# Reordering the attention steps ahead of a mixture-of-experts chain, on one Trainium2 core

## The chip, the cores and the metric

The kernel runs on one core of a Trainium2 chip. The metric is the device time of one execution in microseconds. The kernel before took 670.33 us (median of 3 runs, 669.29 to 670.39). All inputs lie in the chip's memory, and the output goes back there.

## The reference

```python
def _attn_ref(q, k, v):                       # (2, 8, 576, 64) each
    scores = q @ k.T / sqrt(64)               # per batch and head
    mask_local = (rel >= 0) & (rel < 32)      # heads 0 to 3; rel = row - column
    mask_strided = (rel >= 0) & (column % 32 == row % 32)   # heads 4 to 7
    return softmax(where(mask, scores, -1e9)) @ v
def reference(...):
    x = attn_out as (1152 tokens, 512)
    x = sum over 4 experts of p[:, e] * (relu(x @ w1[e]) @ w2[e])     # w1 (512, 1024)
    return (sigmoid(x @ w_gate) * (x @ w_val)) @ w_out                # 1536 wide
```

Matrix products are done with operands split into a high and a low part (three products for one), in fp32r for the first expert and in fp16 after it.

## The kernel before, in words

Tokens lie in three tiles T of 384; a batch has 576 tokens, so batch 0 fills T = 0 and half of T = 1. The first expert's work is cut in "early" units: `early_up(s, T)` and `early_down(s, T)`, each four groups of 12 matmuls (`split_products`, L919). The first four units, all on T = 0, need only batch 0 of the attention. The remaining units follow, with nothing of the attention in them.

Each engine executes its instructions in the order in which the program issues them. The attention is a generator, `attention()` (L867): each `next` issues one numbered step. Steps 0 to 13 (`FIRST_GROUPS` = 14) are issued one after the other; the rest are issued inside the first four early units, 0.3 steps (`ATT_RATE`) after each triple of matmuls. `early_step` issues one step of weight preparation: a cast on ScalarE (ACT, `wh`) or a subtraction on GpSimd (POOL, `wl`).

A batch has ten attention pieces. Eight are local (here l0 to l7: 288 queries of one head each). Two are strided tiles (here s0 and s1: two heads each). Each goes through the same stages: scores on TensorE (PE), maximum on VectorE (DVE), exponent on ACT, sum and reciprocal on DVE, scaling on POOL (L103 is the line of all these, because a helper issues them), transposes on PE (L748, L823), copy out of PSUM, product with the values on PE (L762 strided, L842 local), split of the result into `xh` and `xl`. Two local pieces share one value product; l2, l3, l6, l7 issue it for themselves and their partners.

The order before comes from tables: `SEQUENCE` puts s0 at step 0, l0 to l7 at steps 1 to 8, s1 at step 9; `LOCAL` and `STRIDED` say how many steps behind the scores each stage is issued. Batch 1 has s0 at 15, s1 at 17 and l0 to l7 at 18 to 25. `EMPTY` adds matmuls on zeros (`keep_warm`, L270) to the steps. `head_start` issues the half of an early group that needs only the strided channels.

Small matmuls: a strided score tile is 128 records of 64x18 (L723), a strided value tile 128 of 18x18 (L762). PSUM tiles of the pool `gp` have four slots, shared by transposes, query and key transposes (`qkps`), zeros, strided value tiles and early groups; `op_` has one slot and `sp_` three for scores. Loads are issued by SyncE (SP) in program order, and an issue whose buffer is not free holds up the ones behind it.

Of the kernel before, what the change touches and what calls it, by code (L numbers as in the profile page):

```python
# [9 lines left out]
F32 = mybir.dt.float32  # L10
# [22 lines left out]
PSUM_BUFS = 4  # L33
PB_BUFS = 5
WARM = 11
EMPTY = {0: 4, 1: 4, 2: 4, 3: 3, **{i: 2 for i in range(4, 10)}, 10: 1, 11: 1, 12: 1, 13: 1}
T_BUFS = 4
STEP_US = dict(early_up=0.53, early_down=0.53, expert_up=0.49, expert_down=0.49, gated_up=0.25, gated_down=0.65)
MARGIN = 5.5
# [3 lines left out]
SOON = 0.9  # L43
PARK_BUFS = 4

LOCAL = (("values", 5), ("transpose", 3), ("norm", 1), ("scores", 0), ("max", 0), ("exp", 0), ("split", 5))
STRIDED = (("values", 3), ("transpose", 2), ("scores", 0), ("norm", 1), ("exp", 0), ("split", 3))
SEQUENCE = (("s", 0, 0),) + tuple(("l", 0, x) for x in range(8)) + (("s", 0, 1),)
SECOND = ((15, ("s", 1, 0)), (17, ("s", 1, 1))) + tuple((18 + x, ("l", 1, x)) for x in range(8))
FIRST_GROUPS = 14  # L50
PT_BUFS = 5
VS_BUFS = 1
WEIGHTS_FROM = 5
HEAD_START = (12, 13)
ATT_RATE = 0.3


class Ledger:
# [50 lines left out]
def attn_moe_glu_kernel(ctx, tc, q, k, v, dp, w1, w2, wg, wv, wo, out):  # L109
# [35 lines left out]

    def load_strided_qk(b, c):
        h0 = 4 + 2 * c
        both = accp.tile([NU, 2, 2, 8 * D], F32, tag="acc", name="qk01") if (b, c) == (0, 1) else None
        for x, nm in enumerate(("qs", "ks")):
            if (b, c) == (0, 1):  # L150
                qkv[nm, b, c] = both[:, x]
# [12 lines left out]
    def load_strided_v(b, c):  # L164

        h0 = 4 + 2 * c
        t = atp.tile([128, 16 * D], F32, tag="vs", name="vs", bufs=VS_BUFS)
# [13 lines left out]
    def load_vl(b, half):  # L181
        if ("vl", b) not in qkv:
            qkv["vl", b] = atp.tile([128, 4, 6, D], F32, tag="vl", name="vl")
        t = qkv["vl", b]
        i0, i1 = (1, 3) if half == 0 else (3, 6)
        if half == 0:
            nc.sync.dma_start(t[:, :, 0, :], v[b, 0:4, 0:128, :].rearrange("h p d -> p h d"))
        for h in range(4):
            src = v[b, h, 96 * i0 - 32:, :]
            win = bass.AP(src.tensor, src.offset, [[D, 128], [96 * D, i1 - i0], [1, D]])  # L190
            nc.sync.dma_start(t[:, h, i0:i1, :], win)

    raw, lands = {}, {}
    NJ = F2 // 512
# [478 lines left out]
    def qk_strided(b, c, hh):  # L673

        for nm, dst in (("qs", QT), ("ks", KT)):
# [13 lines left out]
        if (b, c, hh) == (0, 1, 1):  # L689
            acc["x2"] = accp.tile([128, KC, NTOK], F32, tag="acc", name="x2acc")  # L690
        if (b, c, hh) == (1, 1, 1):
            alloc_x(NT - 1)

# [56 lines left out]
        act.copy(t, ps)  # L750
        pt_tiles[g] = t

    def strided_values(g):
        _, b, c = g
        t, vs = pt_tiles.pop(g), qkv["vs", b, c]
        os = [(op_ if b and not j else gp).tile([128, 512], F32, tag="o" if b and not j else "g", name="o")
              for j in range(2)]
        for y in range(16):
# [6 lines left out]
        of_tiles[g] = os  # L765

    def strided_split(g):
        _, b, c = g
        for j, o in enumerate(of_tiles.pop(g)):
            ov = o[:, :16 * NA].rearrange("p (y a) -> p y a", a=NA)  # L770
            for T, off, s0, n in x_parts(b, 0, S):
                a0, a1 = s0 // 32, (s0 + n) // 32
                sel = lambda t: t[T][:, 2 + c, off:off + n].rearrange("p (a j y) -> p j y a", j=2, y=16)[:, j]
                dve.tensor_copy(sel(xh), ov[:, :, a0:a1])
                dve.tensor_tensor(sel(xl), ov[:, :, a0:a1], sel(xh).bitcast(F32), ALU.subtract)

    def local_scores(pair):

# [88 lines left out]
    def attention():  # L867
# [6 lines left out]
        locals_ = [("l", b, c, half, hh) for b in range(B) for half in range(2) for hh in range(2) for c in range(2)]  # L874
        for step, (kind, b, x) in (*enumerate(SEQUENCE), *SECOND):
            for order, (name, behind) in enumerate(STRIDED if kind == "s" else LOCAL):
                if kind == "s":
                    f = dict(values=strided_values, transpose=strided_transpose, scores=strided_scores,
                             norm=strided_norm, exp=strided_exp, split=strided_split)[name]
                    add(step + behind, order, f, (kind, b, x))  # L880
                    continue
                g = locals_[8 * b + x]
                if name in ("scores", "max"):
                    if x % 2 == 0:
                        f = local_scores if name == "scores" else local_max
                        add(step, order, f, locals_[8 * b + x:8 * b + x + 2])
                    continue
                f = dict(values=local_values, transpose=local_transpose, norm=local_norm, exp=local_exp,
                         split=local_split)[name]
                add(step + behind, order, f, g)  # L890
        for step, f, *a in ((0, qk_local, 0, 0), (1, qk_local, 0, 1), (2, qk_local, 0, 2), (7, qk_strided, 0, 1, 0),
                            (8, qk_strided, 0, 1, 1), (14, qk_strided, 1, 0, 0), (14, qk_strided, 1, 0, 1),
                            (15, qk_strided, 1, 1, 0), (16, qk_strided, 1, 1, 1), (17, qk_local, 1, 0),
                            (18, qk_local, 1, 1), (19, qk_local, 1, 2)):
            add(step, 20, f, *a)
        for x, step in enumerate(HEAD_START):
            add(step, 30, head_start, x)
        for step, n in EMPTY.items():
            add(step, 10, keep_warm, n)
        qk_strided(0, 0, 0)  # L900
        keep_warm(2)
        qk_strided(0, 0, 1)
# [389 lines left out]
    with tc.manual_schedule():  # L1292
# [2 lines left out]
        make_constants()  # L1295
        for part in range(3):
            load_local(0, part)
        load_raw_to(1)
        nc.sync.dma_start(ptok, dp.rearrange("(t p) e -> p t e", p=128))
        load_strided_v(0, 0)  # L1300
        load_vl(0, 0)
        load_strided_qk(0, 1)
        load_raw_to(2)
        load_vl(0, 1)
        for T in range(NT - 1):
            alloc_x(T)

        def attend():

            i = next(att, None)  # L1310
            if i == 4:
                load_strided_v(0, 1)
            if i == 6:
                load_raw_to(3)
            if i == 6:
                token_weights()
            if i == 7:
                spread_token_weights()
            if i == 9:
                load_p(0, 0, p00)  # L1320
            if i == 10:
                load_strided_qk(1, 0)
                load_strided_qk(1, 1)
            if i == 12:
                load_strided_v(1, 0)
                load_local(1, 0)
            if i == 13:
                load_local(1, 1)
                load_local(1, 2)
            if i == 14:  # L1330
# [12 lines left out]
        halves = job(x_half())  # L1343
# [21 lines left out]
        for n, u in enumerate(units):  # L1365
# [25 lines left out]
            if n >= N_EARLY:  # L1391
                load_p_some(n)
                load_p_some(n)
                load_some(n)
            ahead[0] = AHEAD["expert" if gated else u[0].split("_")[0]]
            if n >= N_EARLY:
                background(n)
# [47 lines left out]
```

## Time and profile before

| | |
|---|---|
| profiled execution | 669.88 us |
| its span, first to last instruction | 668.1 us |
| mean granted TensorE clock | 0.977 |
| PE busy | 650.3 us (97%) |
| DVE busy | 434.6 us (65%) |
| ACT busy | 323.0 us (48%) |
| POOL busy | 251.0 us (38%) |

Durations are of this one execution. [...] "issue" in the chain of waits is time in which an engine waited for nothing that the profile shows. Times of the trace count from the span's start.

### The profile page before, as it was taken

The numbers are of one execution on the slowest core, as the hardware profiler recorded it, in microseconds if no ns is written. First come the engines' busy times: TensorE is split into PE (matmuls) and PEld (weight loads), VectorE is DVE, ScalarE is ACT, GpSimd is POOL, SyncE is SP. The second block draws the span as 40 slices with busy tenths as digits, with TensorE's granted clock in tenths as the row PEclk, the third lists the DMA queues.
The fourth block names the chain that finished last, engine by engine and source line by source line (L and its number), as shares of the span: only waits on it lengthen the run. The fifth ranks groups of instructions, "written<-read, shape, count | busy, mean of one in ns | idle before, by whom it ended". The sixth has DMA issues, their size and how long they took to land.

```text
span 668.1 us, 13953 instructions
## 1 busy us (share of the span) xinstructions
PE 650.3 (97%) x5615; PEld 480.1 (72%) x5620; DVE 434.6 (65%) x857; ACT 323.0 (48%) x680; POOL 251.0 (38%) x282
## 2 busy tenths in 40 slices
PE   9869899999999999999999999999999999999998
PEld 5558788999876666666666666666988778977794
DVE  4735465678745288666687788898894568733432
ACT  3332324355576464678445636462557455443230
POOL 3361423000043142645044536360265566454541
PEclk9877889999999999999999999999999999999999
DMA  7558330004044064425274464434201842240002
GB/s 169 153 149 195 121 92 1 31 1 127 6 133 134 5 195 144 139 99 186 75 268 159 131 246 149 139 110 156 80 19 63 296 157 85 85 169 1 22 27 95
DMA packets 49080, 77.09 MB, mean 115 GB/s; under 512 B 20020, under 2 KB 24920, under 8 KB 47864
## 3 DMA queue, kind: packets, MB, share of 16 engines
q1 hardware_dynamic: 49016, 76.20, 36.1%
q8 instruction: 44, 0.72, 0.4%
q14 instruction: 20, 0.16, 0.1%
HBM read 59.66 MB, written 16.53 MB: 114 GB/s over the span
## 4 chain that ended last, share of the span: by engine, by line
PE 94%; DVE 3%; issue 1%; ACT 1%; POOL 0%; POOLq 0%; DVEq 0%; ACTq 0%
PE gps L923 23%; PE gps L924 22%; PE gps L925 22%; PE gps L1025 19%; PE o L762 1%; PE warm L270 1%; PE sps L792 1%; PE o L842 1%; PE qkps L702 1%; PE sps L723 1%; DVE xl L103 1%; DVE xh L103 1%; DVE nm L103 1%; PE tps L748 0%; PE tps L823 0%
## 5 line engine op out<-in xcount | busy, mean ns | idle before, releaser
L103 POOL TENSOR_TENSOR hl<-t,hh 128x384 f16<-128x384 f32 x72 | 76.6, 1067 | 180.1 <-ACT t L103 176.3
L1025 PEld LDWEIGHTS <-w 128*128 128x128 f16 x1512 | 125.0, 98 | 1.8
L1025 PE MATMUL gps<-x,w 128*128 128x192 f16 x1512 | 126.2, 246 | 0.0
L923 PE MATMUL gps<-x,w 128*128 128x384 f16 x288 | 93.9, 326 | 0.0
L924 PE MATMUL gps<-x,w 128*128 128x384 f16 x288 | 93.9, 326 | 0.0
L925 PE MATMUL gps<-x,w 128*128 128x384 f16 x288 | 93.9, 326 | 0.0
L923 PE MATMUL gps<-hh,w 128*128 128x384 f16 x288 | 93.9, 326 | 0.0
L924 PE MATMUL gps<-hl,w 128*128 128x384 f16 x288 | 93.9, 326 | 0.0
L925 PE MATMUL gps<-hh,w 128*128 128x384 f16 x288 | 93.9, 326 | 0.0
L923 PEld LDWEIGHTS <-w 128*128 128x128 f16 x576 | 56.4, 98 | 37.3 <-issue 0.2
L925 PEld LDWEIGHTS <-w 128*128 128x128 f16 x576 | 56.4, 98 | 37.2
L924 PEld LDWEIGHTS <-w 128*128 128x128 f16 x576 | 56.4, 98 | 36.4
L103 ACT ACTIVATE hh<-gps 128x384 f16<-128x384 f32 (+1 forms) x96 | 46.8, 487 | 61.4 <-PE gps L925 61.0
L103 POOL TENSOR_TENSOR stage<-magn,stage 128x512 f16<-128x512 f32 x36 | 45.5, 1273 | 45.1 <-ACT magn L103 38.9
L103 ACT ACTIVATE w<-raw,up 128x512 f16<-128x512 f32 x48 | 32.0, 715 | 34.8 <-DVE up L103 34.7
L103 DVE SCALAR_TENSOR_TENSOR w<-raw,up,w 128x512 f16<-128x512 f32 x48 | 40.1, 870 | 5.1 <-ACT w L103 4.9
L103 ACT ACTIVATE bits<-raw 128x512 f32<-128x512 f32 x36 | 24.3, 674 | 38.3 <-DVE magn L103 38.0
L924 PE MATMUL gps<-w,hh 128*128 128x512 f16 (+1 forms) x112 | 41.6, 371 | 0.0
L923 PE MATMUL gps<-w,hh 128*128 128x512 f16 (+1 forms) x112 | 41.6, 371 | 0.0
L925 PE MATMUL gps<-w,hl 128*128 128x512 f16 (+1 forms) x112 | 41.6, 371 | 0.0
L103 POOL TENSOR_TENSOR sg<-four,sg 128x384 f32<-128x384 f32 x9 | 9.9, 1098 | 80.5 <-DVE four L103 80.5
L103 DVE SCALAR_TENSOR_TENSOR t<-gps,comb,pb 128x384 f32<-128x384 f32 x36 | 22.0, 612 | 27.2 <-PE gps L925 26.6
(157 smaller groups left out, 1263.4 us busy)
## 6 DMA issues: line engine op xcount, KB each, us to landing
raw<-in_moe_w_dram SPq DMA_DIRECT2D x32, 512.0 KB
raw<-in_moe_w_gate_dram SPq DMA_DIRECT2D x12, 512.0 KB
raw<-in_moe_w_val_dram SPq DMA_DIRECT2D x12, 512.0 KB
raw<-in_moe_w_out_dram SPq DMA_DIRECT2D x12, 512.0 KB
wg<-stage SPq DMA_DIRECT2D x21, 256.0 KB
wv<-stage SPq DMA_DIRECT2D x21, 256.0 KB
w<-wg SPq DMA_DIRECT2D x3, 1024.0 KB
wo<-stage SPq DMA_DIRECT2D x12, 256.0 KB
```

Of the source, the lines that this page charges most:

```text
L103: return f(*a, **k)
L270: nc.tensor.matmul(ps, zero.to_broadcast([128, 128]), zero.to_broadcast([128, 512]), start=True, stop=True,)
L702: nc.tensor.transpose(ps[:, i * 128:(i + 1) * 128], src[:, 3 * part + i].rearrange("p j d -> p (j d)"), ident,)
L723: nc.tensor.matmul(pv_[32 * i:32 * i + NA, x, :], QT["s", b, c, hh][lo:lo + 64, rp, z, :], KT["s", b, c, hh][lo:lo + 64, rp, z, :], start= ...
L762: nc.tensor.matmul(os[j][hh * 64:hh * 64 + 64, y * NA:(y + 1) * NA], vs[r0:r0 + NA, y * D:(y + 1) * D], t[r0:r0 + NA, col:col + NA], start ...
L792: nc.tensor.matmul(pv_[:, j, :], qs_, ks_, start=False, stop=j == 2)
L842: nc.tensor.matmul(o[x * 64:x * 64 + 64, j * 96:(j + 1) * 96], lhsT, tts[x][:, j, :], start=True, stop=True)
L923: nc.tensor.matmul(ps, ah, bh, start=first and i == 0, stop=False)
L924: nc.tensor.matmul(ps, ah, bl, start=False, stop=False)
L925: nc.tensor.matmul(ps, al, bh, start=False, stop=last and i == n - 1)
L1025: nc.tensor.matmul(o, l_, r_, start=first and x + kk + y == 0, stop=last and x * kk * y == 2, skip_group_check=True)
```

## The change

Steps are listed one by one. In each batch s1 moves from behind the local pieces to step 5, between l3 and l4, and the last stage of batch 0 falls in step 12 (13 before). The strided value product is issued in two halves, in two successive steps; its two PSUM tiles are taken at the first half and given back after the second part of the split, two steps later. The strided split goes by token tile, and its copy into `xh` moves from DVE to ACT. s1's queries, keys and values of batch 0 get space of their own (`stead`), so that its values can be loaded without a wait for s0's; the buffer of the result `x2` is taken later. Several loads move ahead, others back. Zeros per step fall from 31 matmuls in all to 19. Weight preparation in steps 5 to 12 goes at two steps each (16 in all, as before, but evenly). `ATT_RATE` falls from 0.3 to 0.25, and batch 1 starts at step 14.

```diff
-EMPTY = {0: 4, 1: 4, 2: 4, 3: 3, **{i: 2 for i in range(4, 10)}, 10: 1, 11: 1, 12: 1, 13: 1}
+EMPTY = {0: 3, 1: 2, 2: 2, 3: 1, 4: 2, 5: 1, 6: 1, 7: 1, 8: 1, 9: 1, 10: 1, 11: 2, 12: 1}
-FIRST_GROUPS = 14
+SECOND = 14
+FIRST_GROUPS = 13
-HEAD_START = (12, 13)
-ATT_RATE = 0.3
+HEAD_START = (10, 11)
+ATT_RATE = 0.25
...
-    def strided_values(g):
+    def strided_values(g, half):
...
+        if half == 0:
+            of_tiles[g] = [
+                (op_ if b and not j else gp).tile([128, 512], F32, tag="o" if b and not j else "g", name="o")
+                for j in range(2)]
+        os = of_tiles[g]
+        for y in range(8 * half, 8 * half + 8):
...
-    def strided_split(g):
+    def strided_split(g, part):
+        T, off, s0, n = list(x_parts(b, 0, S))[part]
...
-                dve.tensor_copy(sel(xh), ov[:, :, a0:a1])
-                dve.tensor_tensor(sel(xl), ov[:, :, a0:a1], sel(xh).bitcast(F32), ALU.subtract)
+            act.copy(sel(xh), ov[:, :, a0:a1])
+            dve.tensor_tensor(sel(xl), ov[:, :, a0:a1], sel(xh).bitcast(F32), ALU.subtract)
...
+        for b in range(B):
+            z = SECOND * b
+            ls = [("l", b, c, half, hh) for half in range(2) for hh in range(2) for c in range(2)]
+            for c, at in ((0, z), (1, z + 5)):
+                g = ("s", b, c)
+                add(at, 30, strided_scores, g)
+                add(at, 50, strided_exp, g)
+                add(at + 1, 10, strided_norm, g)
+                add(at + 2, 60, strided_transpose, g)
+                add(at + 3, 60, strided_values, g, 0)
+                add(at + 4, 60, strided_values, g, 1)
+                add(at + 4, 90, strided_split, g, 0)
+                add(at + 5, 90, strided_split, g, 1)
+            exps = (1, 2, 3, 4, 6, 7, 8, 9)
+            turns = (4, 5, 6, 7, 9, 10, 10, 11)
+            for x, g in enumerate(ls):
+                if x % 2 == 0:
+                    add(z + exps[x], 30, local_scores, ls[x:x + 2])
+                    add(z + exps[x], 40, local_max, ls[x:x + 2])
+                add(z + exps[x], 50, local_exp, g)
+                add(z + exps[x] + 1, 20, local_norm, g)
+                add(z + turns[x], 10, local_transpose, g)
+            for x, at in ((2, 7), (3, 8), (6, 11), (7, 12)):
+                add(z + at, 5, local_values, ls[x])
+                add(z + at, 90, local_split, ls[x])
+            for part in range(3):
+                add(z + part, 80, qk_local, b, part)
+            for hh in range(2):
+                add(z + 3 + hh, 80, qk_strided, b, 1, hh)
+                if b:
+                    add(z - 1, 80, qk_strided, b, 0, hh)
         for x, step in enumerate(HEAD_START):
-            add(step, 30, head_start, x)
+            add(step, 95, head_start, x)
         for step, n in EMPTY.items():
-            add(step, 10, keep_warm, n)
+            add(step, 70, keep_warm, n)
...
+        load_strided_v(0, 0)
+        load_strided_qk(0, 1)
         load_raw_to(1)
+        load_vl(0, 0)
+        load_raw_to(2)
+        load_strided_v(0, 1)
+        load_vl(0, 1)
         nc.sync.dma_start(ptok, dp.rearrange("(t p) e -> p t e", p=128))
...
-            for _ in range((i >= WEIGHTS_FROM) + (i >= WEIGHTS_FROM + 4) + (i in (11, 12))):
+            for _ in range(2 * (i >= WEIGHTS_FROM)):
                 early_step(0)
```

The second argument of `add` orders the calls inside a step.

## Rows read from the trace of the kernel before

**Rows 1.** The page's 40 equal slices: granted TensorE clock in tenths.

```profile
PEclk9877889999999999999999999999999999999999
```

**Rows 2.** Busy time by stretch: PE, PEld, DVE, ACT, POOL (instructions), clock, DMA share, GB/s.

```profile
8.00:17.00 9.00, 8.53 (x231) 6.49 (x234) 4.88 (x14) 4.35 (x17) 1.50 (x2) 1.00 0.81 162
17.00:35.50 18.50, 15.12 (x199) 9.60 (x194) 13.31 (x38) 8.30 (x40) 7.30 (x8) 0.91 0.54 140
35.50:50.30 14.80, 8.91 (x282) 7.55 (x282) 4.53 (x13) 4.13 (x8) 9.04 (x9) 0.66 0.62 166
50.30:54.95 4.65, 4.25 (x22) 2.75 (x21) 3.93 (x12) 0.00 (x0) 0.00 (x0) 0.50 0.64 143
54.95:120.90 65.95, 62.33 (x888) 56.22 (x888) 35.45 (x93) 22.58 (x79) 21.16 (x24) 0.90 0.36 95
120.90:668.10 547.20, 543.91 (x3983) 393.85 (x3981) 369.91 (x682) 281.55 (x533) 208.39 (x226) 1.00 0.34 114
```

**Rows 3.** Chain that ended last, 35 to 55 us: start, duration, what.

```profile
35.60 1.21 PE sps L723 x80
...
38.84 1.26 POOL wl L103
...
43.93 3.32 PE o L762 x116
47.25 2.51 issue
```

**Rows 4.** The same chain, 16 to 22 us.

```profile
16.27 2.04 PE o L762 x122
...
19.37 0.22 issue
...
20.30 1.02 DVE nm L103 x2
...
21.73 0.02 issue
```

**Rows 5.** DVE's groups by form, 8 to 55 us: busy us, mean ns, idle before.

```profile
L103 DVE COPY PT<-tps 128x288 f32<-128x288 f32 x8 | 3.5, 439 | 0.9 <-PE tps L823 0.9
...
L103 DVE CAST xh<-o 128x192 fp32r<-128x192 f32 x5 | 2.3, 450 | 9.5 <-PE o L762 9.5
...
L103 DVE CAST xh<-o 128x96 fp32r<-128x96 f32 x5 | 1.5, 300 | 0.0
```

**Rows 6.** ACT's groups in the same stretch.

```profile
L103 ACT COPY PTs<-tps 128x512 f32<-128x512 f32 x2 | 1.2, 586 | 3.1 <-PE tps L748 3.1
...
L103 ACT ACTIVATE qsT<-qkps 128x288 f32<-128x288 f32 x2 | 0.8, 410 | 0.0
```

**Rows 7.** The tile `ss` (strided sums), 0 to 100 us: ns minimum, median, maximum.

```profile
L103 DVE TENSOR_SCALAR ss<-ss x4: 174/458/1273, 11.8 to 78.0; 128x16 f32<-128x16 f32 x4
```

**Rows 8.** Busy time around the clock's falls; columns of Rows 2.

```profile
36.90:40.30 3.40, 1.10 (x8) 0.76 (x7) 3.26 (x8) 1.47 (x3) 1.60 (x2) 1.00 0.79 220
40.30:57.30 17.00, 13.16 (x171) 10.57 (x173) 5.55 (x18) 2.66 (x5) 6.85 (x6) 0.50 0.65 168
...
74.50:77.90 3.40, 3.17 (x10) 2.74 (x9) 1.39 (x3) 0.65 (x2) 1.28 (x1) 0.50 0.18 47
77.90:81.35 3.45, 3.45 (x144) 2.97 (x144) 0.57 (x4) 0.00 (x0) 1.90 (x2) 0.99 0.38 134
81.35:84.75 3.40, 3.40 (x14) 3.40 (x14) 3.30 (x9) 2.03 (x8) 0.70 (x1) 0.50 0.22 68
...
91.20:94.60 3.40, 3.40 (x21) 3.19 (x18) 2.67 (x7) 1.15 (x6) 0.00 (x0) 0.55 0.55 98
```

**Rows 9.** PE's waits, 54.95 to 120.9 us: total us, times, longest.

```profile
PE qkps L702 <- issue: 1.9, 1, 1.9
PE tps L748 <- POOL wide L103: 1.2, 1, 1.2
```

**Rows 10.** The chain of waits again, one matmul of an early group.

```profile
57.66 0.17 PE gps L924
```

More of the change, by code (lines that the diff above doesn't have):

```diff
@@ L44 @@
 PARK_BUFS = 4
[L46 to L49, printed above, removed]
-FIRST_GROUPS = 14
+SECOND = 14
+FIRST_GROUPS = 13
 PT_BUFS = 5
-VS_BUFS = 1
 WEIGHTS_FROM = 5
-HEAD_START = (12, 13)
-ATT_RATE = 0.3
+HEAD_START = (10, 11)
+ATT_RATE = 0.25
 class Ledger:
@@ L147, in load_strided_qk @@
         h0 = 4 + 2 * c
-        both = accp.tile([NU, 2, 2, 8 * D], F32, tag="acc", name="qk01") if (b, c) == (0, 1) else None
         for x, nm in enumerate(("qs", "ks")):
             if (b, c) == (0, 1):
-                qkv[nm, b, c] = both[:, x]
+                qkv[nm, b, c] = stead[:NU, 16 * D * x:16 * D * (x + 1)].rearrange("p (h x) -> p h x", h=2)
             elif (b, c) == (1, 1):
@@ L166, in load_strided_v @@
         h0 = 4 + 2 * c
-        t = atp.tile([128, 16 * D], F32, tag="vs", name="vs", bufs=VS_BUFS)
+        if (b, c) == (0, 1):
+            t = stead[:, 32 * D:48 * D]
+        else:
+            t = atp.tile([128, 16 * D], F32, tag="vs", name="vs")
         for x in range(4):
@@ L191, in load_vl @@
             nc.sync.dma_start(t[:, h, i0:i1, :], win)
+    stead = accp.tile([128, KC * NTOK], F32, tag="acc", name="stead")
     raw, lands = {}, {}
@@ L688, in qk_strided @@
                 dve.tensor_copy(t, pv_)
-        if (b, c, hh) == (0, 1, 1):
-            acc["x2"] = accp.tile([128, KC, NTOK], F32, tag="acc", name="x2acc")
         if (b, c, hh) == (1, 1, 1):
@@ L751, in strided_transpose @@
         pt_tiles[g] = t
-    def strided_values(g):
+    def strided_values(g, half):
         _, b, c = g
[L755 to L758, printed above, removed]
+        t, vs = pt_tiles[g], qkv["vs", b, c]
+        if half == 0:
[4 more added lines that the diff above has]
+        for y in range(8 * half, 8 * half + 8):
             for j in range(2):
@@ L764, in strided_values @@
                         vs[r0:r0 + NA, y * D:(y + 1) * D], t[r0:r0 + NA, col:col + NA], start=True, stop=True)
-        of_tiles[g] = os
-    def strided_split(g):
+    def strided_split(g, part):
         _, b, c = g
-        for j, o in enumerate(of_tiles.pop(g)):
+        T, off, s0, n = list(x_parts(b, 0, S))[part]
+        for j, o in enumerate(of_tiles[g]):
             ov = o[:, :16 * NA].rearrange("p (y a) -> p y a", a=NA)
-            for T, off, s0, n in x_parts(b, 0, S):
-                a0, a1 = s0 // 32, (s0 + n) // 32
-                sel = lambda t: t[T][:, 2 + c, off:off + n].rearrange("p (a j y) -> p j y a", j=2, y=16)[:, j]
-                dve.tensor_copy(sel(xh), ov[:, :, a0:a1])
-                dve.tensor_tensor(sel(xl), ov[:, :, a0:a1], sel(xh).bitcast(F32), ALU.subtract)
+            a0, a1 = s0 // 32, (s0 + n) // 32
+            sel = lambda t: t[T][:, 2 + c, off:off + n].rearrange("p (a j y) -> p j y a", j=2, y=16)[:, j]
+            act.copy(sel(xh), ov[:, :, a0:a1])
+            dve.tensor_tensor(sel(xl), ov[:, :, a0:a1], sel(xh).bitcast(F32), ALU.subtract)
     def local_scores(pair):
@@ L872, in add @@
             work.setdefault(step, []).append((order, len(work.get(step, ())), f, a))
[L874 to L895, printed above, removed]
+        for b in range(B):
[29 more added lines that the diff above has]
+                    add(z - 1, 80, qk_strided, b, 0, hh)
@@ L1310, in attend @@
             i = next(att, None)
-            if i == 4:
-                load_strided_v(0, 1)
             if i == 6:
                 load_raw_to(3)
[L1315 to L1321, printed above, removed]
+            if i == 8:
                 load_strided_qk(1, 0)
                 load_strided_qk(1, 1)
+            if i == 9:
+                token_weights()
+                load_strided_v(1, 0)
+            if i == 10:
+                spread_token_weights()
+                load_local(1, 0)
             if i == 12:
-                load_strided_v(1, 0)
-                load_local(1, 0)
-            if i == 13:
+                load_p(0, 0, p00)
                 load_local(1, 1)
                 load_local(1, 2)
-            if i == 14:
+            if i == 13:
                 load_vl(1, 0)
@@ L1394, in attn_moe_glu_kernel @@
                 load_some(n)
+            if u == ("early_down", 0, 0):
+                acc["x2"] = accp.tile([128, KC, NTOK], F32, tag="acc", name="x2acc")
             ahead[0] = AHEAD["expert" if gated else u[0].split("_")[0]]
```

5 lines of the change are left out of this document (removed).

## Prediction

> **What bounds the kernel now.** I read the page's slices first: the granted clock stands at 9 in tenths from the seventh slice on, and the lower digits are all in the first six, some 100 of 668 us [rows 1]. Then the busy time by stretch: from 120.9 us to the end PE is busy 543.91 of 547.20 us at clock 1.00 [rows 2]. That stretch holds nothing of the attention, and its weights are prepared against its own units, so I take it as a block that starts earlier or later. All that the change can move is when the block starts. Ahead of it lie two stages. Stage A, batch 0, runs to the first full early group at 54.95 us; stage B, the four early units with batch 1 among them, takes 65.95 us.
>
> In stage A two engines take turns as the bound. From 17.0 to 35.5 us DVE is busy 13.31 of 18.50 us; from 35.5 to 50.3 only 4.53 of 14.80, and PE 8.91 [rows 2]. The chain of waits says why: s1 comes last and alone. Its scores end at 36.8, its scaling stands behind a weight subtraction on POOL (38.84 to 40.10), its transposes and values then run at clock 0.50 (116 records of the value tile in 3.32 us, against 122 in 2.04 at 16.27), and inside the values PE stands still for 2.51 us with nothing to wait for [rows 3, 4, 8]. I read that stillness as the fetch of PE's own instructions: the value tile is 128 matmuls and 128 weight loads in a row. The same happens for 1.9 us in stage B [rows 9].
>
> In stage B PE is busy 62.33 of 65.95 us, at mean clock 0.90 [rows 2]: the loss is mostly clock.
>
> **The change, stage A.** *DVE's sum.* Before, DVE did 4.88 + 13.31 + 4.53 + 3.93 = 26.65 us in 8 to 54.95 us [rows 2]. The move to ACT takes away four copies of 192 columns and four of 96 in batch 0: 4 x (0.45 + 0.30) = 3.0 us [rows 5]. l7's split, which before lay behind 54.95, belongs to the stage: two copies and two subtractions of about those sizes, 1.5 us. That leaves 25.1 us, 4.9 of it done by 17 us [rows 2]. The rest, 20.2 us in some 58 instructions with 0.03 us between neighbours (an estimate from the 0.02 between two of them in the chain [rows 4]), is 22 us of DVE without a wait.
>
> *Where DVE resumes.* Before, the maxima of l2 and l3 start at 20.30, because their scores are behind the whole value tile (2.04 us) and the wait of 0.22 [rows 4]. The value halves now stand behind the scores, so the maxima start near 20.3 - 2.3 - 0.2 = 17.8. Floor for DVE's last instruction of the stage: 39.8.
>
> *DVE's waits.* I walked the queues step by step in the new order with the durations of these rows. DVE idles for 1.2 us in step 4 (key transposes behind half a value tile and two zeros), 0.9 in step 5 (s1's exponent), 1.25 in step 8 (scores of l6, l7 behind the values of l3, which need the one slot that l2's split gives back), 1.25 in step 9 (s1's `xh` on ACT behind two exponents), 1.1 in steps 11 and 12, and 1.05 in small pieces: 6.75 in all. DVE ends at 46.6, and early_up, which needs only l7's first part, could start 1.1 earlier, at 45.5.
>
> *What the walk leaves out.* First, slots. The two value tiles are now held for two steps, so two of gp's four slots serve all transposes; head_start at step 10 then waits for s1's second split. A wait is at most one copy and one transpose, 0.44 us [rows 5] and about as much for the transposes (an estimate: three records, where three of an early group take 3 x 0.17 [rows 10]); two such waits show in the tail, 2 us; bounds 0 (all hidden) and 8 (one in each of nine steps). Second, POOL. A sum of 16 columns on DVE takes 174 ns, and 1273 at worst, when it meets a weight subtraction (1.26 us) on POOL [rows 3, 7]. Before, half of the subtractions ran while DVE was idle; now all eight run beside it, with some seven such sums. I take 0.5 us that isn't hidden, bounds 0 and 7 x 1.1. Third, instruction fetch: s1's scores (256 records in 1.2 us) follow half a value tile in step 5, with the DMA queues full (share 0.81 and 0.54 in the two stretches [rows 2]). I take 0.5, bounds 0 and 2.51 [rows 3].
>
> [...]
>
> So early_up starts at 45.5 + 2 + 0.5 + 0.5 = 48.5 instead of 54.95: **6.5 us**. Ends: 38.7 with no wait at all (16 us saved), and 45.5 + 8 + 7.7 + 2.5 = 63.7 with every bound against it at once (9 us lost).
>
> *At no cost.* ACT's eight copies per batch of 0.41 to 0.59 us each [rows 6] lie in 8.30 + 4.13 us busy of 33.3 [rows 2]; without that cover they would cost 4 us. Twelve zeros fewer give PE back time that it waits away anyhow. The loads: the initial ones all stand ahead of s1's values (about 34 us in the walk), and the DMA share of 0.54 in 17 to 35.5 [rows 2] shows room; SP then carries batch 1's queries, keys and values past the weight loads, for use from step 13 on. If a load were late, its step waits for it whole, some 3 us. `x2`'s later buffer waits only for s1's values, done ten microseconds earlier.
>
> **Stage B.** The clock is 0.50 in 74.50 to 77.90 and in 81.35 to 84.75 [rows 8], and mostly in 91.20 to 94.60; each costs half of 3.4, 1.7 us. The first follows PE's stillness. Before the second, in 77.90 to 81.35, PE was busy 3.45 of 3.45 us, but with one whole value tile and small local matmuls, no early group [rows 8]; the third is alike. With halves, four triples of an early group (12 x 0.17 = 2.1 us [rows 10]) stand between them. I count both away: 3.4 us. The stillness and its clock, 1.9 + 1.7 = 3.6, came right behind a strided score tile; where it falls depends on how the tile lies in the fetched blocks, and scores aren't cut: half of it, 1.8. The 1.2 us for s0's scaling [rows 9] shrink as steps come every four triples instead of 3.3: 0.6. Against these: in step 22 s1's first half takes the single slot of `op_` one step after l3's values took it, and PE waits until DVE has made the maxima of l6 and l7, 1.02 us [rows 4], and the copies of l3's split, 0.7 [rows 5]: 1.7 us. Sum: 3.4 + 1.8 + 0.6 - 1.7 = **4.1 us**; ends 9.4 (all clock and waits gone, the 1.2 us of half clock at 54.95 to 57.3 too) and -2.
>
> Together 10.6 us: 669.88 - 10.6 = 659.3. The profiled execution lies 0.45 under the median of the runs shown, so **659.7**; this case's own range is 653 to 663.
>
> **Rivals.** *Halves don't hold the clock.* If what counts isn't the small matmuls, the falls at 81.35 and 91.2 come back: 10.6 - 3.4 = 7.2 saved, 663.1. For it: PE at 0.50 also followed a stretch with 1.10 of 3.40 us busy [rows 8], so idle time does it too, and I can't tell the causes apart. Against it: no wait of PE in 77.9 to 81.35.
> [...]
>
> *Half clock in stage A.* PE has fewer zeros and waits of up to 3 us (in the walk, 25.9 to 28.8, for s1's chain on DVE). If the clock falls there and stays, PE's 19 us of steps 4 to 12 (my sum) take 1.7 times as long (as the value tile's records [rows 3, 4]); early_up starts near 53, and 2 + 4.1 are saved: 664.2. Against it: the mean clock was 0.91 in 17 to 35.5, where PE waited for 3.4 us in all [rows 2].
>
> *Slower: PSUM slots.* The value tiles are held through three steps, four times (steps 3 to 5, 8 to 10, 17 to 19, 22 to 24): twelve steps in which transposes, key tiles and, in stage B, early groups queue for the slots that are left. It decides from 1.05 us a step on beyond what I counted (12.6 us). At 1.2 us, a little over one copy and transpose for each, stage A loses 6 more, stage B 8: 4 slower, 673.7. Against it: in stage B only one of the two tiles lies in gp.
>
> *More.* DVE near its floor and stage B without falls: 10 + 9: 651.
>
> **How the numbers follow.** Forecast 0.48, halves 0.18, half clock 0.12, slots 0.13, more 0.09. The range 651 to 668 takes in all but the slots and half of the outer edges. A difference under 0.2% (1.3 us) can't be told from none by these runs. Faster 0.82, same 0.06 (half-clock case at its bad end, slots at its mild end), slower 0.12.
>
> **What would show it.** The first early_up matmul near 48.5 and the first unit on T = 1 (120.9 before) near 110. L762 in groups of 64, with no stillness inside; clock 1.00 behind steps 18 and 23; DVE without a gap of 9.5 us before `xh` [rows 5]; ACT issuing that copy; PE waiting some 1.7 us ahead of the seventh L762 group. It is wrong if early_up starts behind 53, if waits for copies out of PSUM head PE's list, or if the last stretch is longer than 547.2 us.

## The result, and the profile after

The changed kernel takes 663.86 us (median of 9 runs, 659.38 to 666.49), the one before 670.33 beside it (9 runs, 668.57 to 671.37): ratio 0.9907, interval 0.9879 to 0.9935. It is faster by 6.5 us. The profiled execution took 659.38, 10.5 less than before's 669.88, and it is the shortest of the nine; so its trace shows what the change can do, not what it does on the median. The median, 663.86, lies outside the 653 to 663 that the forecast gave as its own range. A second profiled execution of the same kernel (the first experiment) took 663.17, and the difference between the two is told there.

The page's slices of granted clock in the changed kernel, against [rows 1]: lower digits in slices 2, 3 and 6, where they filled slices 2 to 6.

```profile
PEclk9679989999999999999999999999999999999999
```

Busy time by stretch in the changed kernel, with the columns of [rows 2]; the cuts lie at the first matmul of `early_up` (48.14 us) and at the first unit on T = 1 (110.0).

```profile
8.00:17.00 9.00, 8.17 (x191) 6.20 (x178) 5.72 (x16) 4.42 (x18) 2.32 (x3) 1.00 0.88 213
17.00:35.50 18.50, 16.03 (x344) 11.83 (x339) 10.03 (x30) 8.55 (x35) 7.00 (x8) 0.72 0.50 124
35.50:48.10 12.60, 10.59 (x155) 7.90 (x148) 6.69 (x25) 5.89 (x21) 8.49 (x8) 0.73 0.85 211
48.10:110.00 61.90, 58.08 (x883) 52.01 (x882) 33.16 (x85) 24.73 (x87) 21.41 (x24) 0.97 0.41 107
110.00:657.30 547.30, 543.96 (x3983) 393.91 (x3981) 370.47 (x683) 281.58 (x533) 208.03 (x225) 1.00 0.34 114
```

Stage A shrank from 54.95 to 48.1 us, stage B from 65.95 to 61.9, and the last stretch stayed at 547.3 [rows 2]. In the profile of before, 2.51 of those 54.95 us were the stillness inside s1's values [rows 3]; the first profile of the changed kernel has none in stage A, so without stillness the stage went from 52.4 to 48.1. The chain of waits in stage A, where [rows 3] showed s1 alone, now runs, behind the load of s1's keys, through DVE, ACT and PE in turns:

```profile
10.59 7.74 DMA stead<-in_k_dram
18.46 0.49 PE qkps L681 x4
...
33.67 0.46 PE sps L784 x2
34.13 0.88 PE sps L792 x12
35.01 0.55 DVE nm L99
35.64 1.00 ACT P L99 x5
36.76 0.61 ACT wh L99
37.36 1.05 ACT P L99 x6
38.42 0.38 ACT xh L99
38.82 0.88 DVE xl L99 x2
```

PE's waits in stage B of the changed kernel (columns of [rows 9]) have one long entry without a releaser, and the timeline shows where it is: L763, the first half of s1's values in step 22, starts 1.58 us late, when DVE has done two maxima and two copies into `xh` (start, duration, instruction, idle time before it).

```profile
PE o L763 <- issue: 1.6, 1, 1.6
PE gps L932 <- ACT hh L99: 1.1, 1, 1.1
PE gps L932 <- ACT qsT L99: 0.7, 2, 0.5
```

```profile
89.66 0.40 ACT L99 COPY of<-o 128x288 f32<-128x288 f32 x1 [1.41 <-PE o L842]
...
90.85 1.02 DVE L99 TENSOR_REDUCE nm<-sps 96x3 f32<-96x384 f32 x2 [1.61 <-PE sps L792]
...
91.79 0.51 DVE L99 CAST xh<-o 128x192 fp32r<-128x192 f32 x2
...
92.39 1.12 PE L763 MATMUL o<-PTs,vs 18*64 18x18 f32 x64 [1.58 <-issue]
```

Behind that wait PE runs at half clock once:

```profile
93.90:97.20 3.30, 3.30 (x12) 3.20 (x12) 0.00 (x0) 0.00 (x0) 0.00 (x0) 0.50 0.07 17
```

That is one fall in stage B where [rows 8] had three after the stage's first microseconds.

### The profile page after: what moved, and what is told of

Same layout as the page of the kernel before. It is cut to its first block, busy times and chain, and to the rows that moved or that the text cites. A ratio compares the mean times of both kernels' runs of the same rounds, so it can differ in the third digit from the quotient of the medians.

```text
span 657.3 us, 13924 instructions
## 1 busy us (share of the span) xinstructions
PE 644.1 (98%) x5608; PEld 475.6 (72%) x5608; DVE 428.7 (65%) x841; ACT 327.3 (50%) x696; POOL 250.9 (38%) x282
## 4 chain that ended last, share of the span: by engine, by line
PE 92%; DVE 2%; ACT 2%; SPq 1%; DMA 1%; issue 1%; POOL 0%; ACTq 0%; POOLq 0%; DVEq 0%
PE gps L932 23%; PE gps L933 23%; PE gps L934 23%; PE gps L1034 19%; DMA stead<-in_k_dram 1%; SPq L177 1%; PE o L842 1%; PE o L763 1%; ACT P L99 1%; PE sps L792 1%; PE tps L823 0%; DVE ss L99 0%; PE qkps L681 0%; DVE xl L99 0%; PE warm L270 0%
## 5 line engine op out<-in xcount | busy, mean ns | idle before, releaser
L932 PE MATMUL gps<-x,w 128*128 128x384 f16 x288 | 93.9, 326 | 0.0
L933 PE MATMUL gps<-x,w 128*128 128x384 f16 x288 | 93.9, 326 | 0.0
L934 PE MATMUL gps<-x,w 128*128 128x384 f16 x288 | 93.9, 326 | 0.0
L932 PE MATMUL gps<-hh,w 128*128 128x384 f16 x288 | 93.9, 326 | 0.0
L933 PE MATMUL gps<-hl,w 128*128 128x384 f16 x288 | 93.9, 326 | 0.0
L934 PE MATMUL gps<-hh,w 128*128 128x384 f16 x288 | 93.9, 326 | 0.0
L99 POOL TENSOR_TENSOR stage<-magn,stage 128x512 f16<-128x512 f32 x36 | 45.5, 1273 | 45.1 <-ACT magn L99 38.9
```

Source lines behind the costliest of these rows:

```text
L99: return f(*a, **k)
L932: nc.tensor.matmul(ps, ah, bh, start=first and i == 0, stop=False)
L933: nc.tensor.matmul(ps, ah, bl, start=False, stop=False)
L934: nc.tensor.matmul(ps, al, bh, start=False, stop=last and i == n - 1)
```

## The experiments

Edits are against the changed kernel unless said otherwise. "Fetch" stands for PE standing still in a run of small matmuls, or right behind one, with nothing to wait for; that it is the fetch of instructions is a reading, taken up in the second experiment. Ratios are to the kernel before, run beside each experiment: its median was 669.15 us beside the control, the halves together, the split from the copy and the zeros, 670.87 beside the fetch, ACT's copies, s1's place and the scores in halves, and 671.33 beside the rest. A difference of two medians from different groups can be off by some 2 us for that reason.

### What differs between two executions of one kernel

The changed kernel again, with no edit; it serves as the control of the others.

> The changed kernel itself once more, as the control of this call. Its runs so far lie between 659.4 and 666.5 us, and their granted clock between 0.984 and 0.974. Theory (the spread is clock): the time without half of the time at 0.50, span x (1 - (1 - clock)), is the same within 2 us in all runs (646 to 650 us so far), and a profile of a slower run shows more stretches at 0.50 ahead of 110 us. Rival (something else varies, a load or a wait): that corrected time varies as much as the time itself.

Measured: 663.81 (661.47 to 666.13), ratio 0.9918 [0.9888, 0.9947]. Stage A took 51.98 us, 3.8 more than in the other profile; stage B 61.85. PE's timeline and the two totals by stretch (columns of [rows 2]) show the difference:

```profile
21.77 0.62 PE L763 MATMUL o<-PTs,vs 18*64 18x18 f32 x14 [1.18 <-issue]
...
29.15 0.45 PE L721 MATMUL sps<-ksT,qsT 64*18 64x18 f32 x28 [2.77 <-issue]
```

```profile
0.00:21.20 21.20, 18.56 (x342) 12.67 (x344) 9.73 (x26) 9.02 (x33) 6.81 (x19) 0.95 0.85 207
0.00:27.50 27.50, 22.82 (x469) 15.96 (x471) 11.58 (x32) 10.14 (x36) 7.63 (x20) 0.84 0.85 196
51.95:113.80 61.85, 58.02 (x883) 52.01 (x882) 32.05 (x85) 24.76 (x87) 21.44 (x24) 0.97 0.42 110
```

PE stood still for 1.18 + 2.77 = 3.95 us, once after 686 records (matmuls and weight loads) and once after 940, and not at all there in the first profile. 51.98 - 3.95 = 48.0: apart from fetch both executions have the same stage A.

Of the expectation neither side held. Span times granted clock, an estimate of the time without the half of the stretches at 0.50, lies between 646.4 and 649.9 in the nine runs and these four: a spread of 3.5 us, not within 2, where the spans spread by 7.1. But it accounts for three of the four slowest runs (666.05 to 666.13): their clock is 0.974, and 664.0 x 0.974 = 646.7 against 657.3 x 0.984 = 646.8 for the shortest. So fetch makes the difference between the two profiles, and half clock much of that between other runs; where it lies in those, no profile shows.

### Is it the fetch of instructions?

The kernel before, with three warm-up matmuls fewer and 32 of eight columns more, so that all later instructions lie 58 records further on.

```diff
-WARM = 11
+WARM = 8
...
+        tiny = gp.tile([128, 512], F32, tag="g", name="tiny")
+        for _ in range(32):
+            nc.tensor.matmul(
+                tiny[:, :8], zero.to_broadcast([128, 128]), zero.to_broadcast([128, 8]), start=True, stop=True)
```

> The kernel before with 32 matmuls of 8 columns on zeros in place of 3 of 512 in the warm-up: PE's program is 58 records longer ahead of everything, at about the same time. Theory (the stillness inside s1's values is instruction fetch, at a fixed count of PE's records): before it came behind 116 of the tile's 128 matmuls; now it comes 58 records, 29 matmuls, earlier, behind about 87, and the one behind the strided scores of stage B moves in among them. Rival (a load or a buffer ends it): it stays behind 116 matmuls. If the DMA queues happen to be free, it may be too short to be seen.

Measured: 669.99 (one run). `early_up` started at 58.02, 54.5 without the two stalls, where the kernel before has 52.4. The stillness moved, but not by 58 records: it left s1's values and stood in s0's values (L762) and s1's scores (L723). PE's timeline and the totals to those points, then the totals to the two points of the kernel before:

```profile
21.48 0.83 PE L762 MATMUL o<-PTs,vs 18*64 18x18 f32 x21 [2.23 <-issue]
...
42.28 0.27 PE L723 MATMUL sps<-ksT,qsT 64*18 64x18 f32 x12 [1.26 <-issue]
```

```profile
0.00:20.50 20.50, 16.76 (x344) 11.56 (x345) 6.56 (x20) 6.45 (x20) 6.03 (x18) 0.95 0.81 181
0.00:41.90 41.90, 33.90 (x596) 22.42 (x596) 20.56 (x61) 14.76 (x60) 13.42 (x26) 0.88 0.56 134
```

```profile
0.00:48.50 48.50, 39.24 (x717) 26.80 (x721) 25.27 (x70) 18.89 (x68) 21.49 (x33) 0.88 0.67 162
0.00:73.90 73.90, 60.41 (x1095) 45.09 (x1101) 37.83 (x101) 26.15 (x85) 28.47 (x39) 0.86 0.68 166
```

The forecast of the place failed, and what came in its stead says more. Matmuls and weight loads together, the stillness stood at 689 and 1192 here, at 1438 and 2196 before, at 686 and 940 in the control: neighbours 254, 252 and 246 apart, the last step 758, three times 253. The other profiles agree: their thirteen stalls of 0.5 us or more stand at 684 to 688, at 938 to 942 and at 1440 records. The same counts pass without a stall in other executions (in the first profile of the changed kernel and in that of the split from the copy). One packet of 0.02 MB on the queue that the profile calls "instruction" starts in the stall or within some 3 us ahead of it, in each of the five stalls of the kernel before, of the control and of the whole tile without a wait (below), as here in the DMA view of the kernel before, 47.2 to 49.8 us:

```profile
q8 instruction: 1, 0.02, 2.5%
```

Over the whole span that queue has 44 packets in the profile of before and 44 in the first one of the changed kernel, for 11235 and 11216 matmuls and weight loads: one for some 255 records, and the stalls stand on a grid of some 252. They lasted 0.5 to 5.2 us. Such packets also come where PE doesn't stall (one between 17.0 and 18.5 us of the changed kernel's first profile). So the counts and the packets speak for fetch; why it is late in one execution and not in another, no run shows.

### Do the halves hold the clock?

Both halves in one step, behind one another:

```diff
-                add(at + 4, 60, strided_values, g, 1)
+                add(at + 3, 60, strided_values, g, 1)
```

> The second half of each strided value product is issued right behind the first, in the same step; all else as in the changed kernel. Theory (halves hold the clock in stage B): falls to 0.50 follow the two value tiles of batch 1, 1.7 us each, and 3 to 4 us are lost against the control; a stillness inside a tile may add to it. Rival (halves don't hold the clock, the falls come from waits): the time of the control within 1 us, or less, since the split can start a step earlier in effect.

Measured: 666.26 (664.83 to 666.42), ratio 0.9950 [0.9934, 0.9965]: 2.4 us of the gain gone. Stage B 64.25, but the clock held at 1.00 behind s0's whole tile (74 to 81 us) and fell to 0.50 from 97.0 to 103.6, behind the 1.58 us wait and s1's whole tile:

```profile
74.00:81.00 7.00, 5.74 (x40) 5.28 (x39) 3.11 (x9) 2.24 (x10) 0.82 (x1) 1.00 0.23 76
97.00:103.60 6.60, 6.60 (x84) 6.46 (x77) 0.37 (x2) 0.31 (x2) 0.00 (x0) 0.50 0.04 10
```

So one of the two falls that the theory named came, and it lasted longer. Wait and whole tile came together there, so the same edit was made again with the wait removed (its edit is the next experiment's):

> e3 with the value tiles whole: both halves in one step, but no wait for the op_ slot. In e2 the clock fell behind s1's whole tile of batch 1, which followed a wait of 1.58 us, and not behind s0's. Theory now (the tile alone does not bring the clock down, the wait with it does): no fall in stage B, 58 to 60 us for the stage as in e3 (58.6); any loss against e3 lies in stage A. Rival (the prediction's: whole tiles bring it down): falls behind one or both, stage B 1.7 to 5 us longer.

Measured: 663.04 (661.65 to 665.81), ratio 0.9894 [0.9858, 0.9930]. Stage B 61.45 with one fall, at 0.50 from 98.5 to 101.9 us, behind s1's whole tile and with PE not idle ahead of it. In stage A one stall of 5.20 us inside the whole tile of s0 (start, duration, instruction, idle time):

```profile
23.97 0.18 PE L763 MATMUL o<-PTs,vs 18*64 18x18 f32 x1 [5.20 <-issue]
...
95.58 0.90 PE L792 MATMUL sps<-klT,qlT 64*96 64x128 f32 x12
96.41 2.06 PE L763 MATMUL o<-PTs,vs 18*64 18x18 f32 x128
98.39 0.63 PE L932 MATMUL gps<-xh,wh 128*128 128x384 f32 x1
```

```profile
53.25:114.70 61.45, 58.16 (x883) 51.77 (x882) 32.73 (x85) 24.61 (x87) 21.38 (x24) 0.97 0.39 108
```

So the halves hold the clock at s1: stage B's mean clock is 1.00 in the next experiment and 0.97 here. At s0 the clock holds with a whole tile too (1.00 from 74 to 81 us above), so there they do nothing for it. Against the next experiment they are worth 61.45 - 58.60 = 2.85 us in stage B, 1.8 of it PE's busy time and 1.0 its waits. With the slot's wait in place they are worth 64.25 - 61.90 = 2.35. These are differences between one profile each.

### What the slot of `op_` costs

In the local splits of batch 1, DVE's copy into `xh` reads ACT's copy of the result (`of`) instead of the PSUM tile, so that the slot comes free once ACT has copied. In batch 0 nothing changes, because there `of` is the PSUM tile itself.

```diff
-            dve.tensor_copy(dh, o[:, p0:p0 + n])
+            dve.tensor_copy(dh, of[:, p0:p0 + n])
```

> In the local split of batch 1, DVE's copy into xh reads the SBUF copy `of` in place of the PSUM tile, so that the tile of op_ is given back when ACT has copied it. Theory (the 1.58 us of stillness at 90.82 are the wait for that slot, not instruction fetch): it goes, because the slot is free at about 90.06, before the maxima; 1.6 us saved, and up to 1.7 more if the fall of the clock at 93.9 goes with it: 1 to 3.5 us under the control. Rival (it is a fetch): it stays at 1.6 us in the same place. DVE's copies from SBUF may meet POOL and take longer, which would cost nothing on PE.

Measured: 660.74 (656.12 to 662.25), ratio 0.9879 [0.9854, 0.9905]. Its profile has stage A 48.10 without fetch, and stage B:

```profile
48.10:106.70 58.60, 56.34 (x883) 50.38 (x881) 32.66 (x85) 24.69 (x87) 21.40 (x24) 1.00 0.42 113
```

The wait is gone, and with it the half clock: 3.3 us less than 61.90, of which 1.58 is the wait and half of 3.30, 1.65, the clock. That the wait ended with the slot is thereby shown; the profile itself had named no releaser. The other profiles agree: the wait of 1.58 us stands in all seven profiles of the changed kernel and its versions in which DVE reads the PSUM tile, and in none of the five in which it reads the copy.

### Zeros against the half clock of stage A

```diff
-EMPTY = {0: 3, 1: 2, 2: 2, 3: 1, 4: 2, 5: 1, 6: 1, 7: 1, 8: 1, 9: 1, 10: 1, 11: 2, 12: 1}
+EMPTY = {0: 4, 1: 4, 2: 4, 3: 3, **{i: 2 for i in range(4, 12)}, 12: 1}
```

> 32 matmuls on zeros in batch 0's steps in place of 19 (4, 4, 4, 3, then 2 a step), at the places of the changed kernel. Theory (stage A is bound by DVE and waits, and PE at half clock costs in its last part): clock 1.00 for more of 18 to 46 us, early_up 1 to 3 us earlier than 48.1 in a run like the one shown, the spread smaller. Rival (PE is itself near the bound in stage A, busy 12.5 of 14.5 us): early_up 1 to 3 us later, the 13 extra zeros at 0.22 to 0.43 us each standing in front of the attention's matmuls.

Measured: 662.73 (660.03 to 665.26), ratio 0.9901 [0.9869, 0.9933], not to be told from the control. Half clock in stage A fell from 17.1 to 13.6 us; stage A took 49.79, with 2.54 of fetch. So early_up would have started at 47.3 without fetch, 0.8 earlier than in the control. In stage B the clock stayed at 0.50 from 94.3 to 108.0 behind the slot's wait, where 93.9 to 97.2 was all before, and the stage took 66.15 us in place of 61.9:

```profile
94.30:108.00 13.70, 13.63 (x160) 12.84 (x155) 3.44 (x12) 3.04 (x12) 1.33 (x3) 0.50 0.08 12
```

The edit leaves batch 1 alone, so the length of this fall is a second term, of up to 4 us, that differs between executions.

### ACT's copies

```diff
-            act.copy(sel(xh), ov[:, :, a0:a1])
+            dve.tensor_copy(sel(xh), ov[:, :, a0:a1])
```

> The strided split's copy into xh goes back from ACT to DVE, all else as in the changed kernel (control 663.8 us). Theory (DVE bounds stage A): 3.0 us more work on DVE in batch 0, of which what stands in gaps is hidden; early_up 1.5 to 3 us later, 665 to 667. Rival (ACT's queue is the later one: the subtraction waited 1.31 and 0.72 us for the copy behind two exponents): the same or up to 1 us faster.

Measured: 663.90 (662.49 to 665.35), ratio 0.9904 [0.9868, 0.9940]. Stage A 51.37 with 0.68 + 2.77 of fetch, 47.9 without: the move from DVE to ACT is worth nothing that shows, as the rival had it.

### s1's place in batch 0

s1's scores in step 9, behind the local pieces; batch 1 two steps later (edit cut to its core; `head_start` and a load of batch 1 move along, and two zeros come on top).

```diff
-            for c, at in ((0, z), (1, z + 5)):
+            for c, at in ((0, z), (1, z + (5 if b else 9))):
...
-            exps = (1, 2, 3, 4, 6, 7, 8, 9)
-            turns = (4, 5, 6, 7, 9, 10, 10, 11)
+            exps = (1, 2, 3, 4, 6, 7, 8, 9) if b else (1, 2, 3, 4, 5, 6, 7, 8)
+            turns = (4, 5, 6, 7, 9, 10, 10, 11) if b else (4, 5, 6, 7, 8, 9, 9, 10)
```

> In batch 0 alone s1 goes back behind the local pieces (step 9, its split in 13 and 14), l4 to l7 a step earlier, batch 1 from step 16 on; halves, loads, ACT copies, rate and batch 1's order as in the changed kernel; the same 16 steps of weight preparation. Theory (s1's place is the largest term of stage A): its chain stands alone at the end again, early_up 4 to 7 us later than in the control, 668 to 671 us in all. Rival (halves and loads made the gain): within 1.5 us of the control's 663.8.

Measured: 672.0, 673.2, 673.6 and 662.44; with runs so far apart no ratio is given. In the profile (672.0) stage A took 56.68, with 3.3 of fetch, so 53.4 without, and stage B 66.15:

```profile
PE o L763 <- issue: 3.3, 2, 1.6
PE o L842 <- DVE xl L99: 3.0, 1, 3.0
```

```profile
56.65:122.80 66.15, 62.49 (x881) 56.14 (x881) 31.00 (x81) 24.79 (x87) 21.42 (x24) 0.89 0.28 81
```

By this one trace s1's place is worth 53.4 - 48.1 = 5.3 us of stage A, all of the 4.3 that the stage gained without fetch (52.4 to 48.1) and more. Stage B has the order of the changed kernel; its 66.15 us are the long fall once more, at 0.50 from 101.4 to 115.1. The total isn't settled: one run of four was ten microseconds shorter.

### Strided scores in halves, and what adds up

The 128 records of a strided score tile are issued by head; s1's first head goes one step earlier. With the free slot of `op_`:

```diff
+            if hh != part:
+                continue
...
-                add(at, 30, strided_scores, g)
+                add(at - c, 30, strided_scores, g, 0)
+                add(at, 30, strided_scores, g, 1)
```

> e3 (the local split reads the SBUF copy) with the strided scores cut too: s1's 64 matmuls of the first head are issued a step earlier than those of the second, in both batches. Theory (the spread of stage A is instruction fetch: 1.18 us inside the half value tile and 2.77 inside s1's scores in the control's profile): 256 records in 1.2 us become twice 128 two microseconds apart, the stillness inside the scores goes or shrinks under 1 us; median 1 to 3 us under e3's 660.7. Rival (the fetch is late because the queues are full, whatever PE issues): the stillness moves to another place and keeps its size; the time of e3 within 1 us.

Measured: 658.34 (657.1 to 663.73, 6 runs), ratio 0.9842 [0.9801, 0.9882]. Fetch 0.71 + 0.52 in stage A (50.17), stage B 58.75 at clock 1.00; both stalls are under 1 us, as the theory had it. The same edit without the free slot:

> The changed kernel with the strided scores in halves, the local split reading PSUM again. Separates the two parts of e8. If fetch and slot wait are two terms that add up: the control's 663.8 less e8's step against e3 (2.4 us), 661 to 662, with the wait of 1.6 us in front of s1's first half in batch 1. If e8's step came from something else: 663 to 664.

Measured: 661.67 (660.62 to 661.78), ratio 0.9868 [0.9843, 0.9894]; fetch 2.16, the slot's wait and the fall back, stage B 61.8. By the medians the two edits add up: about 2 us for the scores (663.81 to 661.67), about 3 for the slot. For the slot the stages B show it (58.6 to 59.1 us without the wait, 61.8 to 62.1 with it and 66.15 with the long fall behind it). For the scores the traces don't show how: the stall of 2.16 stood inside the first half of s1's scores, and fetch in stage A was 1.06 to 2.19 us in the four profiles with halved scores against 0 to 3.95 in the six with whole scores and halved value tiles.

With the scores in halves, the free slot and the zeros of the earlier experiment:

> e8 (scores in halves, split from the SBUF copy) with the 32 zeros of e4. Theory (in stage A half clock costs on the way to early_up): the stretches at 0.50 ahead of 48 us shrink from some 20 us to 13, as in e4, and early_up comes 1 to 2 us earlier than e8's 50.2; median 656 to 658. Rival (the zeros stand in front of what the path needs, and add records to the fetched blocks): e8's 658.3 or up to 2 us more.

Measured: 657.87 (655.76 to 661.2, 6 runs), ratio 0.9819 [0.9792, 0.9847]. This is the fastest version, ahead of both kernels; the interval overlaps that without the zeros, so what these add is open. In its profile, the longest of the six runs, early_up started at 53.03 with 2.19 of fetch, later and not earlier than 50.17. Last, weight preparation from step 4 instead of 5 (without the zeros):

```diff
-WEIGHTS_FROM = 5
+WEIGHTS_FROM = 4
...
-            for _ in range(2 * (i >= WEIGHTS_FROM)):
+            for _ in range(2 * (WEIGHTS_FROM <= i < 12)):
```

> e8 with the 16 steps of weight preparation in steps 4 to 11 in place of 5 to 12. Theory (the transposes of l6 wait 1.3 us for a scaling that stands behind a weight subtraction on POOL, and ACT's copies behind casts): POOL and ACT are freer at the end of stage A, early_up 0.5 to 1.5 us earlier, 657 to 658. Rival (the same queues are only blocked a step earlier, at s1's chain): the same or up to 1 us slower.

Measured: 660.70 (657.27 to 663.54), ratio 0.9857 [0.9827, 0.9887]: no gain that shows. Stage A took 53.22 with 1.06 of fetch, the clock at 0.50 from 23.5 to 50.8 us without a break.

## Why the prediction was right, and where it was not

*The number.* In the first profile stages A and B shrank by 6.8 and 4.05 us, against 6.5 and 4.1 forecast, and its time came within 0.1 us of the 659.3 forecast for a profiled execution. That is partly luck: it is the shortest of nine runs and has no fetch in stage A. The median, 4.2 us over the forecast, lies beside the 663.1 and 664.2 of the two rivals on the clock, though neither of these is what the traces show, as told below.

*The block.* Right: the last stretch is 547.20 before and 547.30 after, so all of the gain is an earlier start.

*Stage B, 4.1 us.* 65.95 - 61.90 = 4.05, and 4.10 in the control. Split into waits and clock the forecast holds too: its terms for waits come to 1.7 less half of 1.9 and less 0.6, next to nothing, and PE's waits went from 3.62 to 3.82 us while its busy time fell from 62.33 to 58.08. The single parts came less close. Clock 1.00 behind step 18; behind step 23 one fall remained, and the row of 3.30 us at 0.50 shows it. The stillness of 1.9 us and s0's wait of 1.2 [rows 9] are gone whole, more than the 1.8 + 0.6 counted. The slot wait, forecast at 1.7 in step 22, was 1.58 in that place. Not counted were waits of early groups for ACT, 1.1 + 0.7 us, and the fall behind the slot's wait. The half clock at the stage's start, 1.2 us, went too and stood only in the ends. So errors of some 1 to 2 us each cancelled. The case that halves don't hold the clock is half refuted: it is true of s0, false of s1. For the price, the two stages B without the slot's wait differ by 2.85 with one fall, against 3.4 forecast for two; and the fall behind a whole tile (0.50 from 98.5 to 101.9 us) came with no wait of PE's from 93.7 us on, as that at 81.35 came behind 3.45 us busy of 3.45 [rows 8].

*Stage A, 6.5 us.* Forecast start of `early_up` 48.5; 48.14 in the first profile, 51.98 in the control. The step that failed is the third of "what the walk leaves out": fetch "I take 0.5, bounds 0 and 2.51". What it measured:

| kernel | early_up starts | fetch | difference |
|---|---|---|---|
| changed, first profile | 48.14 | 0 | 48.1 |
| changed, control | 51.98 | 3.95 | 48.0 |
| halves together | 51.17 | 3.03 | 48.1 |
| split from the copy | 48.10 | 0 | 48.1 |
| copies on DVE | 51.37 | 3.45 | 47.9 |
| scores in halves alone | 50.47 | 2.16 | 48.3 |
| whole tile, no wait | 53.29 | 5.20 | 48.1 |
| scores in halves, free slot | 50.17 | 1.23 | 48.9 |
| more zeros | 49.79 | 2.54 | 47.3 |
| scores in halves, free slot, zeros | 53.03 | 2.19 | 50.8 |
| scores in halves, free slot, weights earlier | 53.22 | 1.06 | 52.2 |

The changed kernel, its control and the split from the copy have one and the same stage A, and give 48.0 to 48.1 without fetch, against 48.5 - 0.5 = 48.0 forecast: the walk's sum stands. The next four lie within 0.4 us of one another; the last four do not, and three of them change the zeros or the weights of the stage. The term itself is 0 to 5.2 us, one or two stalls of 0.5 to 3 each and once one of 5.2. I had bounded it by the one stall seen in the trace of before; the shifted run of that kernel had 2.23 + 1.26 in its stage A, so the bound was too low there already. With 3.95 in place of 0.5 the forecast would be 663.1, and the median is 663.86. The nine runs have no profile each, so that fetch makes their whole spread (659.4 to 666.5) isn't shown, and their clocks speak against it; the control shows it for the 3.8 us between the two profiled executions. The second term that differs between executions, the length of the fall behind the slot's wait (3.3 to 13.7 us), the prediction had put at nothing.

*Right sum, wrong split.* "DVE's sum" had DVE busy for 20.2 us from 17 us on, and its walk had it idle for 6.75. It was busy 10.03 + 6.69 = 16.72 of 31.1 us and so idle for some 14. PE was busy 26.62 of 31.1, at a mean clock of 0.72: nearer to the bound than DVE. So the rival "half clock in stage A" did occur in its clock (about 17 us at 0.50), without its price: `early_up` started at 48.1, not near 53. The run with weights earlier comes near that price: there the clock stayed at 0.50 for 27.3 us, and `early_up` started at 53.22, 52.2 without fetch. Whether the clock or the weights' place did it, that run can't tell. The copies on ACT, which I counted as 3.0 us off DVE, brought nothing when put back, as befits an engine with that much idle time. That errors in DVE's work and DVE's waits cancelled is luck of the walk, not a confirmation of DVE as the bound. By its chain the stage is bound by the alternation shown above; more zeros, or the copies put back on DVE, each move it by under what the runs can tell.

*At no cost.* Nearly: the load of s1's keys stands in the chain with 7.74 us and held PE for 0.6 us. POOL's term was small, near the 0.5 taken: `ss` took 982 ns at worst (1273 in [rows 7]), some 0.8 more than its 174, and the eight of the local pieces' sums 164 on average.

```profile
L99 DVE TENSOR_SCALAR ss<-ss x4: 174/536/982, 11.0 to 83.0; 128x16 f32<-128x16 f32 x4
```

*PSUM slots.* The slower rival did not come: of waits for the four slots of `gp` the longest in stage A is 0.6 us, zeros behind a copy of `PT`, where the forecast had taken 2. But one of the signs of error did appear: waits for a slot that DVE still reads head PE's list, 1.3 us in stage A (l3's values behind l2's split) and the 1.58 in stage B. Both are the one slot of `op_`, and both were in the forecast, as DVE's wait of 1.25 in step 8 and as 1.7 in step 22. The 1.3 us of the transposes (L823) are put down to POOL's scaling in other profiles, not to a slot. Two roundings of the prediction, which its sum does not use, are off: 12 x 0.17 is 2.0, and twelve steps at 1.2 us are 14.4, so that this rival would give 674.1.

```profile
PE o L842 <- DVE xl L99: 1.3, 1, 1.3
PE tps L823 <- ACT wh L99: 1.3, 1, 1.3
PE qkps L681 <- DMA stead<-in_k_dram: 0.6, 1, 0.6
PE warm L270 <- DVE PT L99: 0.6, 1, 0.6
```

Open: why a stall comes in one execution and not in the next; why half clock after the same wait in stage B lasted 3.3 or 13.7 us; what half clock in stage A costs; the total with s1 behind; what zeros add; by what the halved scores gain.

## What to carry to other kernels

Profile the same kernel twice before sizing a wait that no engine causes: here one term was 0 in one execution and 3.95 us in the next, and subtracting it made the two agree to 0.1 us. A forecast of a median should not be judged by one execution. Long runs of tiny matmuls are worth cutting where larger work can stand between them: halved values brought 2 to 3 us of stage B here, at one of two places, and halved scores about 2 us in the medians. A PSUM tile that a later reader could take from its copy should be let go with the copy: that line was worth 3 us.

## What the runs showed of the hardware

- The nineteen stalls that no engine or load ended stand at certain counts of PE's own records, some 252 apart (near 686, 940, 1192, 1438 and 2196), in or right behind runs of small matmuls, and last 0.5 to 5.2 us; the same kernel shows them in one execution (3.95 us) and not in another (0).
- The clock fell to 0.50 behind a run of 128 matmuls of 18x18 with PE busy before it (98.5 to 101.9 us of the whole tile without a wait), and did not fall behind the same run at s0 (1.00 from 74 to 81 us of the halves together).
- A wait for a PSUM slot can show as "issue", with no releaser; only taking it away (1.58 us, 3.3 with the clock behind it) named it. The wait for the same slot in stage A showed DVE as its releaser (1.3 us).
- Behind the same wait of 1.58 us the clock stayed at 0.50 for 3.3 us in four profiles and for 13.7 in two; stage B took 61.8 to 62.1 us with the one and 66.15 with the other.
